# Both score products of an odd step ahead of the second mixing, query transposes in even steps, and half of the block relayouts issued by SyncE

## The chip, the cores and the metric

The kernel runs on one core of a Trainium2 chip. TensorE (PE; PEld is its weight load) multiplies into PSUM, which is eight banks of 128 partitions by 512 float32. VectorE (DVE) and ScalarE (ACT) read PSUM and write the on-chip memory SBUF; GpSimd (POOL) works in SBUF alone. SyncE (SP), ACT and POOL issue the transfers (DMA) between SBUF and the device's main memory or inside SBUF. Each engine works through its own list of instructions in order and waits on semaphores for the others. The metric is the time of one execution in microseconds (us).

## The reference

Attention with mixing of heads before and after the softmax ("talking heads") for 4 batches, 12 heads, 448 positions and head size 64, then a feed-forward layer:

```python
scores = scale * np.matmul(q, k.transpose(0, 1, 3, 2))
scores = np.einsum('bhij,hg->bgij', scores, w_pre)
scores = scores - np.max(scores, axis=-1, keepdims=True)
attn = np.exp(scores)
attn = attn / (np.sum(attn, axis=-1, keepdims=True) + 1e-09)
attn = np.einsum('bhij,hg->bgij', attn, w_post)
attn_out = np.matmul(attn, v)
x = np.ascontiguousarray(attn_out.transpose(0, 2, 1, 3)).reshape(B * S, H * D)
h = x @ w_in
g = s * np.maximum(h, 0.0) ** 2 + b
return g @ w_out
```

`w_in` is 768 by 2048, `w_out` 2048 by 768, x has 1792 rows; all is float32.

## The kernel before, in words

The kernel has an attention stage (steps 0 to 89 of one loop, and a tail) and a feed-forward stage that keeps PE full; the change touches the attention alone.

**Chunks, pairs, blocks.** Each batch's 448 query rows are cut into chunks of 120, 120, 120 and 88 rows: 16 chunks, `ci`. For a chunk and a pair of heads `p` (six pairs), `qk` (line 506) multiplies transposed queries `Tq` by transposed keys `Tk` into two PSUM banks `sc`, and `s_copy` (line 519) has ACT copy them, scaled, into the chunk's score tile `S` in SBUF. A *block* is ten query rows with their twelve heads. `relayout(t)` (line 593) is a DMA that carries block t from `S` (rows on partitions) into a tile `blk`, in which the 120 pairs of row and head lie on partitions. There are eight `blk` tiles, and two blocks (an even t and the odd one after it) make a *step* s.

**A step on PE.** `premix` (line 601) multiplies the step's two blocks by `wpre` into two banks `pm`: the first mixing of heads. DVE takes row maxima (`st`, line 617), ACT the exponentials `e` with their sums (line 623), POOL and DVE make from the sums the weights `W` (lines 629, 634, 636). `postmix` (line 638) of step s-2 multiplies `e` by `W` into two banks `po`, the second mixing, and `evacuate` (line 656) has DVE copy both banks into `A`. In even steps `av` and `av_last` (lines 529, 541) multiply `A` by `v` for two head pairs into `xp`; ACT and DVE copy that out, POOL adds, and SP stores the result `xd` (line 588).

**The odd and the even step.** PE's order in a step is the order of the loop's code: `premix`; `av` (even steps), transposes `tr`, `av_last`; one `qk` of the kind "more" (odd steps); `postmix`; one `qk` of the kind "qk" (odd steps, a few even ones). There are 8 banks in four slots of two: `pm` alternates between slots A and B, `xp` and the "more" scores use the one of A and B that the step before has left, `po` has slot C, and the second `qk` and the transposes share slot D. So `postmix` of a step can begin only when DVE has copied the `po` of the step before, and in an even step `xp` can begin only when ACT has read the odd step's `pm`.

**What sets the order around it.** A table `plan` (lines 667 to 748) gives the step of every `qk`, transpose, `av` and load. Query transposes of a chunk (`tr_q`, line 481) stand in the last odd step that is at least one step ahead of the chunk's first `qk`; key transposes (`tr_keys`) in even steps. The copies of the second `qk` are put off to the head of the next step (list `scopies`). At a step's end the relayouts for step s+4 are issued (LDS is 4), then the loads of the plan, then the stores `xd`. In the stretch before the loop, even blocks go to SP and odd ones to POOL; in the loop all go to POOL's queue. SP issues every other load of the attention stage. Each DMA of SP also waits for the one eight DMAs back on its queue.

Of the kernel before, what the change touches and what calls it, by code (L numbers as in the profile page):

```python
# [22 lines left out]
def talking_heads_attention__then__act_relu2_kernel(  # L23
# [13 lines left out]
    nc = tc.nc  # L37
    B, H, S, D = q.shape
# [4 lines left out]
    NP = H // 2  # L43
# [21 lines left out]
    NCH = len(chunks)  # L65
# [15 lines left out]
    LDS, NBLK, LAG = 4, 8, 2  # L81
# [187 lines left out]
    def one(tag, name):  # L269
        return ps.tile([P, 512], F32, tag=tag, name=name, bufs=1)  # L270

    def slot(tag, name):
        return [one(f"{tag}{i}", f"{name}_{i}") for i in range(2)]

    def next_slot(name):
        tag = slots[turn["slot"] % len(slots)]
        turn["slot"] += 1
        return slot(tag, name)
# [227 lines left out]
    def qk(ci, p, sc):  # L506

        b, n0, n = chunks[ci]
        if p == 0:
            s_t[ci] = sp.tile([CH, H, S], F32, tag=f"S{ci % 3}", name=f"S_{ci}")  # L510
        qt, kt = q_t[ci % 2], k_t[b, p]
        for c0, c1 in ((0, 64), (64, CH)):
            for e in range(2):
                nc.tensor.matmul(  # L514
                    sc[e][c0:c1, :S], qt[64 * e:64 * e + 64, p, c0:c1], kt[64 * e:64 * e + 64, :],
                    start=True, stop=True,
                )

    def s_copy(ci, p, sc, apart=False):
        n = chunks[ci][2]  # L520
        s = s_t[ci]
        if apart:
            nc.scalar.activation(s[:n, 2 * p, :], sc[0][:n, :S], AF.Copy, scale=SCALE)
            nc.vector.tensor_scalar_mul(s[:n, 2 * p + 1, :], sc[1][:n, :S], SCALE)
        else:
            for e in range(2):
                nc.scalar.activation(s[:n, 2 * p + e, :], sc[e][:n, :S], AF.Copy, scale=SCALE)  # L527
# [65 lines left out]
    def relayout(t):  # L593
        ci, r, ni = blocks[t]
        nb = first[ci + 1] - first[ci]
        queue = nc.gpsimd if t >= 2 * LDS or t % 2 else nc.sync
        queue.dma_start(  # L597
            blk_t[t % NBLK][R0:R0 + ni * H, :], s_t[ci][r:r + nb * (ni - 1) + 1:nb, :, :]
        )

    def premix(s):
        pm = pm_t[s] = slot("AB"[s % 2], f"pm_{s}")
        for c in range(2):
            blk = blk_t[(2 * s + c) % NBLK]
            for b in range(2):
                k = slice(0, 64) if b == 0 else slice(64, 64 + U)
                nc.tensor.matmul(  # L607
                    pm[b][64 * c:64 * c + 64, :S], wpre[k, :], blk[k, :], start=True, stop=True
                )
# [17 lines left out]
    def totals(s):  # L627
        e, st = e_t[s]
        nc.gpsimd.tensor_scalar(st[:, 4:6], st[:, 2:4], 1e-9, None, op0=ALU.add)
# [39 lines left out]
    plan = {}  # L669

    def at(step, kind, *what):
        plan.setdefault((step, kind), []).append(what)

    LAST_QK = first[NCH - 1] // 2 - LDS - 1
    where = {}
# [4 lines left out]
    for s in range(1, LAST_QK + 1):  # L680
        for kind in ("more", "qk") if s % 2 else ("qk",):
            if n < len(pairs) and (s % 2 or n < len(pairs) * s / LAST_QK):
                ci, p = where["qk", n] = pairs[n]
# [6 lines left out]
    def place(jobs, room):  # L690
        left = 0
        for s in range(NS + LAG + NP + 1):
            left = room(s, left)
            for job in sorted((j for j in jobs if j[0] <= s), key=lambda j: j[1]):
                lo, hi, cost, key, kind, what = job
                if left > 0 or hi <= s:
                    jobs.remove(job)
                    assert s <= hi, job
                    left -= cost
                    where[key] = s  # L700
                    at(s, kind, *what)
        assert not jobs

    jobs = []
    for ci in range(2, NCH):
        s = where[ci, 0]
        where["tr", ci] = max(s - 2 + (s + 1) % 2, 0)
        at(where["tr", ci], "tr", tr_q, ci, 0, NP)
        b = chunks[ci][0]
        if chunks[ci - 1][0] != b:  # L710
            for p in range(0, NP, 2):
                hi = where[ci, p] - 1
                jobs.append((max(where[ci - 1, p + 1] + 1, hi - 3), hi, 1, ("tr", b, p), "tr", (tr_keys, b, p)))
    place(jobs, lambda s, left: s % 2 == 0)

    jobs = []
    for ci in range(NCH):
# [71 lines left out]
    for p in range(NP):  # L789
        sc = next_slot(f"sc_0_{p}")  # L790
# [10 lines left out]
    for p in range(NP - 2):  # L801
        sc = next_slot(f"sc_1_{p}")
        qk(1, p, sc)
        s_copy(1, p, sc, True)

    scopies = []
    NDONE = NS + LAG
    for s in range(NDONE + NP + 1):
        def todo(kind):
            return plan.pop((s, kind), [])  # L810

        while scopies:
            s_copy(*scopies.pop(0))
        if s == LAST_QK + 1:
            early.close()
            rp = ctx.enter_context(tc.tile_pool(name="rp", bufs=1, side="right", reuse_waits="tile"))
            rp.tile([P, S], F32, tag="xraw", name="place_xraw", bufs=NKC)
            rp.tile([P, X_GAP // 4], F32, tag="gap", name="gap_x", bufs=1)
            rp.tile([P, 2, S], F32R, tag="x", name="place_x", bufs=NKC)
            rp.tile([P, END_GAP // 4], F32, tag="end", name="gap_end", bufs=1)  # L820
        other = "AB"[(s + 1) % 2]
        if s < NS:
            premix(s)
        for _ in range({LAST_QK + 5: 4, LAST_QK + 7: 4, LAST_QK + 9: 4, NS + 1: 3, NS + 2: 3}.get(s, 0)):
            head_piece()
        users = {}

        def take(tag, name):
            for _, f in users.pop(tag, []):
                f()  # L830
            users[tag] = []
            return slot(tag, name)

        outputs = todo("av")
        if outputs:
            assert len(outputs) <= 2
            tag = other if s < NS else "B" if s < NS + LAG else "CB"[s % 2]
            outputs = [(*o, xp) for o, xp in zip(outputs, take(tag, f"xp_{s}"))]
            for output in outputs:
                av(*output)  # L840
        for f, *args in todo("tr"):
            for o, x in f(*args, take("D", f"tr_{s}")):
                turn["copy"] += 1
                i = turn["copy"] % 2
                users["D"].append((1 + i, partial((on_act, on_dve)[i], o, x)))
        if outputs:
            av_last(outputs)
            users[tag] += x_copies(outputs)
        for ci, p in todo("more"):
            tag = "D" if outputs else other  # L850
            sc = take(tag, f"sc_{ci}_{p}")
            qk(ci, p, sc)
            users[tag].append((3, partial(s_copy, ci, p, sc)))
        copies_due = sorted(sum(users.values(), []), key=lambda x: x[0])
        if s < NS:
            open_softmax(s)
            maximum(s, 0)
            if s % 2 == 0:
                exponential(s, 0)
        if 0 <= s - 1 < NS:  # L860
            weights(s - 1)
        if s < NS:
            maximum(s, 1)
        for n, f in copies_due:
            if n < 4:
                f()
        if s < NS:
            if s % 2:
                exponential(s, 0)
            exponential(s, 1)  # L870
        due = 7 * NU_EARLY * (s - CONV0) / (LAST_QK - 2 - CONV0)
        while s % 2 == 0 and turn["ops"] < min(due, 7 * NU_EARLY):
            turn["ops"] += 1
            convert_step(NU_EARLY)
        if LAG <= s < NS + LAG:
            postmix(s - LAG)
            for t in (2 * (s - LAG), 2 * (s - LAG) + 1):
                evacuate(t)
        for ci, p in todo("qk"):
            sc = slot("D", f"sc_{ci}_{p}")  # L880
            qk(ci, p, sc)
            scopies.append((ci, p, sc))
        for n, f in copies_due:
            if n == 4:
                f()
        if s < NS:
            totals(s)
        if s + LDS < NS:
            for t in (2 * (s + LDS), 2 * (s + LDS) + 1):
                relayout(t)  # L890
        for f, *args in todo("load"):
            f(*args)
        store_x(0)
        i = s - LAST_QK - 1
        if 0 <= i < NKC:
            load_x(0, 0, i)
        if 2 <= i < NKC + 2:
            split_x(0, 0, i - 2)
            low_parts()
        for kc in (2 * (i - NKC), 2 * (i - NKC) + 1):  # L900
            if 0 <= kc < NKC:
                load_x(0, 1, kc)
            if 4 <= kc < NKC + 4:
                split_x(0, 1, kc - 4)
                low_parts()
        for _ in range(4 if s >= NS else 0):
            convert_step(NU_EARLY + 3)
# [18 lines left out]
    for r in range(NR):  # L926
# [5 lines left out]
        last = {b: i for i, (b, f) in enumerate(order)}  # L932
# [87 lines left out]
```

## Time and profile before

| | |
|---|---|
| median of 3 runs | 836.83 us (831.28 to 839.35) |
| the profiled execution | 836.27 us, its span 834.6 us |
| PE busy | 814.5 us (98%) |
| DVE, ACT, POOL busy | 533.9, 432.6, 327.6 us |
| chain that ended last | PE 91%, DVE 3%, DMA 2%, "issue" 2%, ACT 1%, POOL under 0.5% |
| attention loop | step 0 at 20.6 us, step 89 at 359.5 us |

Matmuls overlap in the array and their ends are modelled, so PE reads as busy where it only waits inside a run of matmuls; what a stretch costs is read from the starts of its runs. "Issue" is time in which an engine waited for nothing that the profile shows.

### The profile page before, as it was taken

The numbers are of one execution on the slowest core, as the hardware profiler recorded it, in microseconds if no ns is written. First come the engines' busy times: TensorE is split into PE (matmuls) and PEld (weight loads), VectorE is DVE, ScalarE is ACT, GpSimd is POOL, SyncE is SP. The second block draws the span as 40 slices with busy tenths as digits, with TensorE's granted clock in tenths as the row PEclk, the third lists the DMA queues.
The fourth block names the chain that finished last, engine by engine and source line by source line (L and its number), as shares of the span: only waits on it lengthen the run. The fifth ranks groups of instructions, "written<-read, shape, count | busy, mean of one in ns | idle before, by whom it ended". The sixth has DMA issues, their size and how long they took to land.

```text
span 834.6 us, 27353 instructions
## 1 busy us (share of the span) xinstructions
PE 814.5 (98%) x11288; PEld 680.6 (82%) x11288; DVE 533.9 (64%) x1182; ACT 432.6 (52%) x1015; POOL 327.6 (39%) x631
## 2 busy tenths in 40 slices
PE   8988998999999999999999999999999999999998
PEld 4556666666666766689999999999999999999998
DVE  6556677687777787889713999390079329947111
ACT  4755676677667676538687731211186877200000
POOL 4556677587756777725332410000033324100000
PEclk9999999999999999999999999999999999999999
DMA  6998379756994477623422335353114302445331
GB/s 147 218 212 211 125 194 216 180 185 173 225 206 156 148 207 196 212 85 94 158 66 67 83 89 161 118 163 134 42 37 144 104 1 77 149 146 185 97 95 48
DMA packets 116483, 115.88 MB, mean 139 GB/s; under 512 B 67892, under 2 KB 105256, under 8 KB 116360
## 3 DMA queue, kind: packets, MB, share of 16 engines
q1 hardware_dynamic: 92976, 64.79, 29.7%
q0 software_dynamic: 14240, 37.75, 15.6%
q10 hardware_dynamic: 9144, 11.60, 3.9%
q8 instruction: 89, 1.46, 0.7%
q14 instruction: 34, 0.28, 0.1%
HBM read 58.99 MB, written 16.52 MB: 90 GB/s over the span
## 4 chain that ended last, share of the span: by engine, by line
PE 91%; DVE 3%; DMA 2%; issue 2%; ACT 1%; POOL 0%; SPq 0%; DVEq 0%; POOLq 0%
PE po L337 28%; PE ph L289 26%; PE po L650 8%; PE sc L514 7%; PE pm L607 7%; PE xp L536 7%; PE xp L551 2%; PE ph_head L289 1%; DMA blk<-S 1%; DVE A L661 1%; PE tr L457 1%; DMA nk<-in_k_dram 1%; PE tr L488 1%; DVE st L617 1%; PE busy L760 0%
## 5 line engine op out<-in xcount | busy, mean ns | idle before, releaser
L623 ACT ACTIVATE e<-pm,st 128x448 f32<-128x448 f32 x180 | 113.2, 635 | 31.4 <-DVE st L634 27.6
L617 DVE TENSOR_REDUCE st<-pm 128x1 f32<-128x448 f32 x180 | 108.9, 610 | 31.5 <-PE pm L607 14.5
L597 POOL DMA_DIRECT2D blk<-S x176 | 108.0, 614 | 32.1 <-issue 10.2
L650 PEld LDWEIGHTS po<-W,e 60*64 60x64 f32 x5040 | 93.6, 136 | 28.3 <-issue 15.9
L661 DVE COPY A<-po 128x420 f32<-128x420 f32 x180 | 98.4, 588 | 28.5 <-PE po L650 27.6
L527 ACT ACTIVATE S<-sc 120x448 f32<-120x448 f32 (+1 forms) x172 | 84.5, 548 | 44.5 <-PE sc L514 44.2
L650 PE MATMUL po<-W,e 60*64 60x60 f32 x5040 | 99.1, 220 | 7.2 <-issue 6.6
L514 PE MATMUL sc<-Tk,Tq 64*56 64x448 f32 (+1 forms) x768 | 98.8, 549 | 4.0 <-issue 2.5
L607 PE MATMUL pm<-blk,wpre 64*64 64x448 f32 (+1 forms) x720 | 94.3, 546 | 2.4 <-issue 0.9
L337 PE MATMUL po<-w,g 128*128 128x384 f32 x504 | 94.2, 336 | 0.0
L305 POOL TENSOR_TENSOR big<-h,big 128x448 fp32r<-128x448 f32 x24 | 30.8, 1283 | 154.7 <-ACT big L304 154.7
L636 POOL TENSOR_SCALAR W<-kron,st 128x60 f32<-128x60 f32 x180 | 82.1, 469 | 20.2 <-DVE st L634 13.4
L305 POOL TENSOR_TENSOR g<-h,g 128x448 fp32r<-128x448 f32 x40 | 49.1, 1228 | 103.3 <-ACT g L304 92.0
L289 PE MATMUL ph<-x,w 128*128 128x448 f32 x432 | 88.1, 362 | 0.0
L337 PEld LDWEIGHTS po<-w,g 128*128 128x128 f32 x504 | 88.0, 188 | 0.0
L289 PEld LDWEIGHTS ph<-x,w 128*128 128x128 f32 x432 | 81.0, 187 | 5.5
L536 PEld LDWEIGHTS xp<-A,v 128*64 128x64 f32 x1152 | 55.7, 136 | 31.9 <-ACT e L623 19.0
L289 PE MATMUL ph<-x,big 128*128 128x448 f32 x378 | 77.6, 362 | 0.0
L289 PEld LDWEIGHTS ph<-x,big 128*128 128x128 f32 x378 | 70.9, 188 | 4.8
L536 PE MATMUL xp<-A,v 128*64 128x120 f32 (+1 forms) x1152 | 66.0, 263 | 0.6 <-DVE A L661 0.5
L337 PE MATMUL po<-big,g 128*128 128x384 f32 x336 | 65.1, 336 | 0.0
L344 ACT ACTIVATE ob<-po 128x384 f32<-128x384 f32 x28 | 13.8, 493 | 97.8 <-PE po L337 86.1
(89 smaller groups left out, 1252.7 us busy)
## 6 DMA issues: line engine op xcount, KB each, us to landing
blk<-S POOLq DMA_DIRECT2D x168, 210.0 KB, 4.2
raw<-in_moe_w_in_dram SPq DMA_DIRECT2D x32, 384.0 KB
raw<-in_moe_w_out_dram SPq DMA_DIRECT2D x32, 384.0 KB
xraw<-xd SPq DMA_DIRECT2D x48, 224.0 KB
part<-ob ACTq DMA_DIRECT2D x28, 192.0 KB
acc<-part SPq DMA_DIRECT2D x28, 192.0 KB
out_dram<-acc ACTq DMA_DIRECT2D x28, 192.0 KB
xd<-xs SPq DMA_DIRECT2D x72, 60.0 KB
```

Of the source, the lines that this page charges most:

```text
L289: nc.tensor.matmul(ph[:, :S], w[:, i, c0:c0 + P], x[:, y, :], start=(kc == 0 and m == 0), stop=(kc == NKC - 1 and m == 2),)
L337: nc.tensor.matmul(po[:, :NO], g[:, x, c0:c0 + P], w[:, y, :], start=(f == 0 and m == 0), stop=(f == NF - 1 and m == 2),)
L514: nc.tensor.matmul(sc[e][c0:c1, :S], qt[64 * e:64 * e + 64, p, c0:c1], kt[64 * e:64 * e + 64, :], start=True, stop=True,)
L527: nc.scalar.activation(s[:n, 2 * p + e, :], sc[e][:n, :S], AF.Copy, scale=SCALE)
L536: nc.tensor.matmul(xp[64 * e:64 * e + 64, :2 * m].rearrange("q (b n) -> q b n", b=2), vt[:, e, c, :], a[:, c:c + NC:NC - 1, 2 * p + e, :m] ...
L597: queue.dma_start(blk_t[t % NBLK][R0:R0 + ni * H, :], s_t[ci][r:r + nb * (ni - 1) + 1:nb, :, :])
L607: nc.tensor.matmul(pm[b][64 * c:64 * c + 64, :S], wpre[k, :], blk[k, :], start=True, stop=True)
L617: nc.vector.tensor_reduce(out=e_t[s][1][:, b:b + 1], in_=pm_t[s][b][:, :S], axis=AX.X, op=ALU.max, negate=True)
L623: nc.scalar.activation(e[:, b, :], pm_t[s][b][:, :S], AF.Exp, bias=st[:, b:b + 1], accum_out=st[:, 2 + b:3 + b])
L636: nc.gpsimd.tensor_scalar(w[:, b, :], kron2, st[:, 6 + b:7 + b], None, op0=ALU.mult)
L650: nc.tensor.matmul(po[r][64 * c:64 * c + 64, m * U:m * U + U], e[64 * r:64 * r + U, b, j0:j0 + 64], w[64 * r:64 * r + U, b, :], start=True ...
L661: nc.vector.tensor_copy(a_t[ci].rearrange("q m h j -> q (m h) j")[:, :, UI * r:UI * r + UI], po_t[t // 2][t % 2][:, :n].rearrange("q (m i) ...
```

## The change

Three edits. The first: `second(s)`, a function that holds what stood behind `postmix`, is called in odd steps without `av` ahead of the copies and so ahead of `postmix`; in even steps it stays where it was. The second: query transposes go to the last free even step ahead of the chunk's first `qk` (free: no key transposes there, and behind the last use of the buffer). The third: in the whole loop even blocks are issued by SP and odd ones by POOL.

```diff
     def relayout(t):
         ci, r, ni = blocks[t]
         nb = first[ci + 1] - first[ci]
-        queue = nc.gpsimd if t >= 2 * LDS or t % 2 else nc.sync
+        queue = nc.gpsimd if t % 2 else nc.sync
...
         s = where[ci, 0]
-        where["tr", ci] = max(s - 2 + (s + 1) % 2, 0)
-        at(where["tr", ci], "tr", tr_q, ci, 0, NP)
...
+    for ci in range(2, NCH):
+        last = where[ci - 2, NP - 1] if ci > 3 else -1
+        where["tr", ci] = max(
+            s for s in range(last + 1, where[ci, 0]) if s % 2 == 0 and (s, "tr") not in plan
+        )
+        at(where["tr", ci], "tr", tr_q, ci, 0, NP)
...
+    def second(s):
+
+        for ci, p in plan.pop((s, "qk"), []):
+            sc = slot("D", f"sc_{ci}_{p}")
+            qk(ci, p, sc)
+            scopies.append((ci, p, sc))
...
             qk(ci, p, sc)
             users[tag].append((3, partial(s_copy, ci, p, sc)))
+        if s % 2 and not outputs:
+            second(s)
         copies_due = sorted(sum(users.values(), []), key=lambda x: x[0])
...
             postmix(s - LAG)
             for t in (2 * (s - LAG), 2 * (s - LAG) + 1):
                 evacuate(t)
-        for ci, p in todo("qk"):
-            sc = slot("D", f"sc_{ci}_{p}")
-            qk(ci, p, sc)
-            scopies.append((ci, p, sc))
+        if s % 2 == 0 or outputs:
+            second(s)
```

**PE in step 41**, an odd step, from its last `premix` matmul on (`pm_41` is the first mixing, `sc_9_0` and `sc_9_1` two score products of chunk 9, `po_39` the second mixing, 28 matmuls). Before:

```order
L607 MATMUL pm_41_1_3770<-blk3_139,wpre_101 64x448
L514 MATMUL sc_9_0_0_3775<-Tk_2_0_3003,Tq1_135 64x448
L514 MATMUL sc_9_0_1_3776<-Tk_2_0_3003,Tq1_135 64x448
...
L650 MATMUL po_39_0_3794<-W_39_3711,e_39_3619 64x60
L650 MATMUL po_39_1_3795<-W_39_3711,e_39_3619 64x60
...
L514 MATMUL sc_9_1_0_3826<-Tk_2_1_3004,Tq1_135 64x448
L514 MATMUL sc_9_1_1_3827<-Tk_2_1_3004,Tq1_135 64x448
```

and now:

```order
L607 MATMUL pm_41_1_3763<-blk3_139,wpre_101 64x448
L514 MATMUL sc_9_0_0_3768<-Tk_2_0_3013,Tq1_135 64x448
L514 MATMUL sc_9_0_1_3769<-Tk_2_0_3013,Tq1_135 64x448
...
L514 MATMUL sc_9_1_0_3775<-Tk_2_1_3014,Tq1_135 64x448
L514 MATMUL sc_9_1_1_3776<-Tk_2_1_3014,Tq1_135 64x448
...
L650 MATMUL po_39_0_3793<-W_39_3709,e_39_3617 64x60
L650 MATMUL po_39_1_3794<-W_39_3709,e_39_3617 64x60
...
L607 MATMUL pm_42_0_3837<-blk4_140,wpre_101 64x448
```

The second product has moved ahead of the second mixing, whose next neighbour is now the first mixing of step 42.

**SP's queue at the head of the loop** (`blk` rows are relayouts, `nq`, `nk` and `v` loads of queries, keys and values). Before, from the last relayout ahead of the loop on:

```order
L597 DMA blk6_142<-S_0_273 120x1x448
L443 DMA nq_3_535<-in_q_dram 80x4x64
...
L443 DMA nq_3_535<-in_q_dram 8x4x64
L427 DMA nk_1_0_602<-in_k_dram 64x8x64
...
L427 DMA nk_1_1_605<-in_k_dram 64x6x64
L402 DMA v_0_685<-in_v_dram 64x2x256
```

and now:

```order
L597 DMA blk6_142<-S_0_273 120x1x448
L597 DMA blk0_136<-S_0_273 120x1x448
L597 DMA blk2_138<-S_0_273 120x1x448
L443 DMA nq_3_535<-in_q_dram 80x4x64
...
L597 DMA blk4_140<-S_1_429 120x1x448
L443 DMA nq_4_602<-in_q_dram 112x4x64
...
L597 DMA blk6_142<-S_1_429 120x1x448
L427 DMA nk_1_0_676<-in_k_dram 64x8x64
```

Every step has one relayout on SP now, and the loads stand between them; in all, 86 relayouts leave POOL's list and enter SP's. On DVE, ACT and PE no instruction is added or taken away: apart from the second products, only the transposes of 13 chunks and their copies have moved, each from an odd step to an even one.

## Rows read from the trace of the kernel before

**Rows 1.** The page: queue (packets, MB, busy share), chain, POOL issues (us, ns), us to landing.

```profile
q0 software_dynamic: 14240, 37.75, 15.6%
...
PE 91%; DVE 3%; DMA 2%; issue 2%; ACT 1%; POOL 0%; SPq 0%; DVEq 0%; POOLq 0%
...
L597 POOL DMA_DIRECT2D blk<-S x176 | 108.0, 614 | 32.1 <-issue 10.2
...
blk<-S POOLq DMA_DIRECT2D x168, 210.0 KB, 4.2
```

**Rows 2.** Windows: stretch, length, busy time of each engine, granted clock, DMA share, GB/s.

```profile
20.00:58.00 38.00, 34.80 (x706) 20.36 (x700) 23.03 (x52) 25.97 (x69) 21.39 (x48) 1.00 1.03 215
...
80.00:100.00 20.00, 17.53 (x438) 11.83 (x440) 11.43 (x29) 11.05 (x32) 11.52 (x27) 0.91 0.46 137
```

**Rows 3.** Timeline of PE: start, us, line, tile, count; the step starts 86.56 and 328.25.

```profile
86.56 1.10 PE L607 MATMUL pm<-blk,wpre 64*64 64x448 f32 x8
...
328.25 0.94 PE L607 MATMUL pm<-blk,wpre 64*64 64x448 f32 x8
```

**Rows 4.** Timeline of PE, steps 65 and 66, and the start of 67.

```profile
273.88 0.98 PE L607 MATMUL pm<-blk,wpre 64*64 64x448 f32 x8
274.69 0.93 PE L514 MATMUL sc<-Tk,Tq 64*64 64x448 f32 x8
275.44 0.99 PE L650 MATMUL po<-W,e 60*64 60x60 f32 x56
...
277.01 0.93 PE L607 MATMUL pm<-blk,wpre 64*64 64x448 f32 x8
277.87 1.45 PE L536 MATMUL xp<-A,v 128*64 128x120 f32 x24
...
279.53 1.00 PE L650 MATMUL po<-W,e 60*64 60x60 f32 x56
280.37 0.96 PE L607 MATMUL pm<-blk,wpre 64*64 64x448 f32 x5
```

**Rows 5.** The chain that ended last, 86.5 to 328.3 us: its shares by line.

```profile
by line: PE sc L514 20.3%; PE po L650 19.5%; PE pm L607 18.6%; PE xp L536 18.3%; PE xp L551 5.8%; DVE A L661 3.3%; PE tr L457 2.7%; issue 2.4%; PE tr L488 2.1%; DVE st L617 1.3%; DVE Tk L502 0.9%; DVE raw L192 0.8%; DVE xr L502 0.7%; DVE xs
```

**Rows 6.** Timeline of PE and DVE, step 41 and the start of 42.

```profile
180.50 0.98 PE L607 MATMUL pm<-blk,wpre 64*64 64x448 f32 x8
...
182.06 1.31 PE L650 MATMUL po<-W,e 60*64 60x60 f32 x53
...
184.86 1.45 PE L536 MATMUL xp<-A,v 128*64 128x120 f32 x24
...
181.24 1.09 DVE L661 COPY A<-po 128x420 f32<-128x420 f32 x2
```

**Rows 7.** Timeline of ACT, step 65.

```profile
275.67 0.98 ACT L527 ACTIVATE S<-sc 120x448 f32<-120x448 f32 x2 [1.34 <-PE sc L514]
...
277.66 0.22 ACT L623 ACTIVATION_READ_ACCUMULATOR e<-pm,st 128x1 f32 x1
277.75 0.99 ACT L527 ACTIVATE S<-sc 120x448 f32<-120x448 f32 x2
```

**Rows 8.** Timeline of SP's queue: relayouts, and the first and last of its next 16 rows.

```profile
17.07 5.86 SPq L597 DMA_DIRECT2D blk<-S  x4
23.03 4.30 SPq L443 DMA_DIRECT2D nq<-in_q_dram  x6
...
55.76 0.72 SPq L414 DMA_DIRECT2D v<-in_v_dram  x1
```

**Rows 9.** Timeline of SP's queue, the first and last of 20 rows, 132 to 162 us.

```profile
132.88 0.39 SPq L137 DMA_DIRECT2D raw<-in_moe_w_in_dram  x1
...
158.87 3.38 SPq L443 DMA_DIRECT2D nq<-in_q_dram  x6
```

**Rows 10.** The chain that ended last, 20 to 86.6 us: start, us, what.

```profile
36.77 6.95 DMA blk<-S
...
80.68 2.31 issue
```

## What the change does to the time: the prediction

> **What bounds the kernel now.** I began with the chain that ended last on the page: PE holds 91% of it and POOL under 0.5% [rows 1]. A faster POOL is thus worth nothing by itself, and the 108.0 us in which it issues relayouts lie beside PE's work. The feed-forward stage is PE's alone, and the change does not touch it; a gain or a loss in the attention goes through to the end unaltered.
>
> Then the attention, 86.56 to 328.25 us, steps 16 to 79 in the profile [rows 3]. The chain over these 241.7 us holds, beside PE's own lines, 3.3% of DVE's copies `A` (8.0 us), 2.4% of "issue" (5.8 us) and some 4% of other DVE work [rows 5]. So PE is the bound, and DVE's copy of `po` is the largest wait. What that looks like is seen in two pairs of an odd and an even step. In steps 65 and 66 nothing is late: first mixing to next first mixing is 3.13 us in the odd step (273.88 to 277.01) and 3.36 us in the even one, 6.49 us for the pair [rows 4]. In step 41 the second mixing starts at 182.06, while DVE copies the step before's `po` from 181.24 to 182.33; its 53 matmuls spread over 1.31 us, against 0.99 us for all 56 in step 65 [rows 4, 6]. From the first mixing to `xp` of the even step it takes 4.36 us there (180.50 to 184.86) [rows 6] and 3.99 us in step 65 (273.88 to 277.87) [rows 4].
>
> ACT stands close behind. `xp` of the even step takes the slot of the odd step's `pm`, so it waits for the odd step's last exponential: its accumulator is read out by 277.88, and `xp` starts at 277.87 [rows 4, 7]. ACT comes there from the copy of the "more" scores, which starts 1.79 us after the first mixing [rows 7]. This chain is 4.0 us long, whatever PE does between.
>
> **The change part by part.**
>
> *Second product ahead of the second mixing.* No instruction is added. The odd step's second mixing starts 0.75 us later: first mixing 0.81, two products at 0.75 each, so 2.3 us into the step in place of 1.56 (step lengths from the starts in [rows 4]). In step 41 the copy `A` ends 1.83 us into the step (182.33 less 180.50) [rows 6], so it would no longer be waited for. PE's new odd step is 0.81 + 0.75 + 0.75 + 0.83 = 3.14 us, with 0.83 for second mixing to first mixing (279.53 to 280.37 [rows 4]): no shorter than the tight step before. The edit thus pays only where `A` is late, and only down to ACT's 4.0 us: 0.36 us in step 41. Of the 32 odd steps of the stretch, 13 show this picture, with 4.27 to 4.92 us from first mixing to `xp`, transposes aside; those behind a key transpose are the latest, and ACT holds them to about 4.27. Together I read 5 us from them. Bounds: 8 late copies of 1.0 us stand on the chain (8.0 us); if all of it came back, 8.0, and if each gave only step 41's 0.36, 2.9. I take 5, which the steps themselves give.
>
> What is late next: `A` of the odd step is now copied beside the first mixing of the even step, so the even step's first row maximum, behind it on DVE, starts about 0.2 us later. The exponential that waits for this maximum stands on ACT behind the copy of the second scores, which begins only when the odd step's exponentials are done (277.75) and takes 0.99 us [rows 7]; that covers it. Without this cover it would cost 0.2 us in 40 steps, 8 us. The order of these copies on ACT does not change, and slot D, which the second product needs 0.8 us earlier, was emptied at the head of the step before.
>
> *Query transposes in even steps.* The same matmuls and copies, 13 times, at another place: the odd step loses them, the even step gets them. In an even step they delay ACT's and DVE's later work, as key transposes do now, and the following odd step gets 0.2 us longer by ACT's chain. In the odd step before they cost as much. Net 0, between -1 and +2 (0.15 us for each of 13).
>
> *Relayouts on SP.* POOL loses 86 issues of 614 ns [rows 1], 53 us off the chain: 0. A relayout has to land four steps later, some 13 us of which the landing takes 4.2 [rows 1]; in steady steps that covers SP's queue. The place to look at is 23 to 57 us. There SP's 16 rows of loads sum to 32.0 us of the 33.4 between first and last [rows 8], the DMA share is 1.03 [rows 2], and the chain waits on a relayout that takes 6.95 us [rows 10]. Four relayouts took SP 5.86 us, 1.47 each [rows 8]. Nine more are 13.2 us; SP falls 12 us behind by the end, against a cover of four steps of 4.0 us less 6.95 for the landing and 0.9 for the first mixing, 8.2 us. So up to 3.8 us late there. But part of SP's 32 us is itself waiting for full DMA engines, and loads that no longer run ahead leave room for relayouts; the other bound is a gain of 1 us. I take +2.
>
> *Behind the relayout on SP* stand the loads and the stores `xd`. Loads of keys and queries are planned two or three steps ahead of their transposes, 7 to 10 us; a lag of 3 or 4 us in steady steps stays below that. In 132 to 162 us SP's 20 rows sum to 26.0 us of 29.4 [rows 9]; eight relayouts add 11.8 and leave a lag of 8.4 us, below the 11 us of four steps of 4.1 less issue and a landing of 4.2.
>
> Sum: 836.27 (the profiled execution; its span is 834.6) - 5 + 0 + 2 = 833.3. That execution lies 0.6 us below the median of the runs; I say **833**.
>
> **Rivals.**
>
> *Nothing comes back (837 us).* ACT's chain is 4.0 us where PE's new path is 3.14 + 0.86 = 4.0 us: they are equal. If DVE's 0.2 us reaches ACT after all, or the startup's 3.8 us is paid in full, the 5 us are gone: 833.3 + 3.8 = 837. For it: the equality in step 65. Against: 13 late steps have slack to give.
>
> [...]
>
> *The pauses go too (826 us).* PE also pauses where the profile names no wait: 5.8 us in the stretch [rows 5], and 2.31 us at 80.68 [rows 10], after which the granted clock is 0.91 in 80 to 100 us, the lower of its two levels (1.2 GHz) for some 3.6 us (1.8 us lost) [rows 2, 10]. They come while transfers are dense. Smaller packets and another order of loads may thin them out; if two thirds of these 9.9 us went, 833 - 7 = 826. They may as well grow.
>
> *SP becomes the bound (850 us).* If a relayout holds SP for about 1.9 us or more, as the slower of the four may have, SP's queue in 132 to 162 us outgrows its cover: (29.4 - 26.0 + 11) / 8 = 1.8 us is the point from which it decides. At 2.3 us, first mixings wait in the startup (32.0 + 9 x 2.3 - 33.4 - 8.2 = 11 us) and in three stretches like that of [rows 9] (26.0 + 8 x 2.3 - 29.4 - 11 = 4 us, of which half is made up between them): 833 - 2 + 11 + 6, about 850, counting 2 us for a lower clock behind long waits. For it: 1.47 us is a mean with a full queue. Against: SP's queue idles most of the time elsewhere.
>
> **How the numbers follow.** Forecast (830 to 836) 0.48; nothing or ten engines (837) 0.24, of which ten engines 0.10; pauses go (826) 0.16; SP bound (850) 0.12. About 1% (8.4 us) is what a measurement of this kernel tells from no change: the three runs before span 8.1 us. Faster than 828.5 is most of the pauses' case and a little of the forecast: 0.17. Slower than 845.2 is the SP case: 0.12. Between: 0.71. The range leaves out the SP case and the far end of the pauses' case, and takes in the bounds of the gain (8.0) and the startup (+3.8) with pauses 4 us either way: 825 to 842.
>
> **What would show it.** Right: 53 matmuls of the second mixing in odd steps back at 0.99 us or less, `A` under 1% of the chain from step 16 to 79, the first mixing to `xp` near 4.0 us in the 13 steps, step 79 reached 4 to 6 us sooner after step 16. Third edit: SP's relayouts near 1.2 us each, no first mixing waiting for `blk` after 60 us. Wrong: `xp` waiting for ACT by 0.2 us or more in most odd steps, or first mixings that wait for `blk`; step 16 starting over 4 us later than 86.56 means the startup was mis-sized.

## The result: 0.7% slower, and the profile after

The changed kernel takes 840.50 us (median of 20 runs, 832.61 to 844.54), the kernel before 834.29 us in as many runs beside it (830.04 to 839.35): 1.0073 times as long, with a 95% interval of 1.005 to 1.0095. The forecast was 833 us, a gain. The profiled execution has 841.25 us, its span 839.5 us, 4.9 us more than that of before.

The page of the kernel after, with the rows that answer to [rows 1]; for a DMA queue: packets, MB, busy share of 16 engines:

```profile
q0 software_dynamic: 7360, 19.31, 7.5%
...
PE 90%; DMA 5%; DVE 1%; issue 1%; SPq 1%; ACT 1%; POOL 0%; ACTq 0%; DVEq 0%; POOLq 0%
...
L597 POOL DMA_DIRECT2D blk<-S x90 | 58.2, 648 | 34.6 <-issue 16.8
...
blk<-S POOLq DMA_DIRECT2D x86, 210.0 KB, 4.1
```

DVE (3% before) and "issue" (2%) are down to 1% each of the chain that ended last, and transfers have come in: 5% against 2%. The same is read from the chain by line, 86.5 to 330 us of the kernel after, which answers to [rows 5]:

```profile
by line: PE pm L607 20.3%; PE po L650 20.2%; PE sc L514 19.2%; PE xp L536 18.0%; PE xp L551 5.5%; DMA blk<-S 4.4%; PE tr L488 3.3%; PE tr L457 3.1%; DMA nk<-in_k_dram 1.8%; issue 0.9%; DVE A L661 0.5%; DVE xs L502 0.4%; SPq L597 0.4%; POOL
```

The copy `A` fell from 3.3% to 0.5%, so the first edit did what it was to do. What is new are blocks (`blk`) and keys (`nk`). Here are the late transfers in the chain from 60 to 365 us of the kernel after (start, us, what), with SP's own time ahead of the keys; ahead of 60 us, in the stretch of [rows 10], the chain has transfers in both kernels:

```profile
65.23 1.37 SPq L427
...
67.44 5.05 DMA nk<-in_k_dram
...
160.12 0.85 SPq L597
161.69 4.49 DMA nk<-in_k_dram
...
244.15 5.80 DMA blk<-S
...
325.69 4.92 DMA blk<-S
```

Before, no transfer stood in the chain between 43.8 and 360 us. The two transfers of keys follow pieces of SP's own time: they left late. How late the second keys of the batch come is seen in SP's queue. First the loads of keys of step 36 in the kernel before (start, us, engine, line, tile, count):

```profile
151.15 1.56 SPq L427 DMA_DIRECT2D nk<-in_k_dram  x2
...
153.95 2.02 SPq L427 DMA_DIRECT2D nk<-in_k_dram  x2
```

and the same loads after, with what stands around them:

```profile
155.60 0.82 SPq L597 DMA_DIRECT2D blk<-S  x1
156.53 1.30 SPq L427 DMA_DIRECT2D nk<-in_k_dram  x2
157.92 2.11 SPq L588 DMA_DIRECT2D xd<-xs  x2
160.12 0.85 SPq L597 DMA_DIRECT2D blk<-S  x1
161.02 1.85 SPq L427 DMA_DIRECT2D nk<-in_k_dram  x2
```

The second pair of loads leaves 7.1 us later (161.02 against 153.95), about what eight relayouts at 0.85 us take. From 134 us on SP has no gap of over 0.4 us there. PE reaches step 36 2.8 us earlier than before, and in its timeline after stands for 4.68 us in the middle of the key transposes:

```profile
161.12 0.52 PE L457 MATMUL tr<-ident,nk 128*128 128x128 f32 x3 [0.22 <-DMA nk<-in_k_dram]
166.32 1.28 PE L457 MATMUL tr<-ident,nk 128*128 128x128 f32 x5 [4.68 <-DMA nk<-in_k_dram]
```

Behind this stand the granted clock falls. The window of 140 to 180 us (length, busy time of PE, PEld, DVE, ACT, POOL, granted clock, DMA share, GB/s), before and then after:

```profile
140.00:180.00 40.00, 37.48 (x916) 25.42 (x912) 28.56 (x70) 26.22 (x73) 25.88 (x58) 1.00 0.74 193
```

```profile
140.00:180.00 40.00, 35.10 (x853) 24.27 (x845) 26.98 (x67) 24.55 (x71) 18.88 (x45) 0.96 0.65 183
```

The granted clock is 0.96 of full in it: the trace has 3.4 us at the lower level (0.50 of full in a window of 166.3 to 169.6 us) from 166.2 us on, as the wait ends; the same comes at the waits for the keys of step 12 (6.8 us, from 70.7 us on) and for the block of step 58 (3.4 us, from 251.6 us on). That is 13.6 us at half speed in the attention, at most 6.8 us lost (in 2.0 us of them PE stood waiting in any case), against at most 1.7 us before. The trace gives the level as a share, not in GHz; an estimate of the rate comes from the feed-forward stage of the kernel before, where at full clock 672 matmuls of 384 columns take 116.48 us and 576 of 448 columns 115.60: 64 columns more take 27.4 ns, 2.34 columns a ns, and half of that is 1.17.

Step by step, from the first weight load of one first mixing to that of the next, the 4.9 us come about so (us after less us before):

```
start of step 0 to step 16     +0.6   step 12 +5.2 and 13 +1.1 (keys, half clock), step 15 -4.7 (a pause of before is gone)
step 16 to step 79             +0.8   step 36 +6.0 (keys), 57 and 58 +4.6 (block of step 58, half clock);
                                      31, 53 and 76 together -4.2 (pauses gone); the 57 others -5.6
step 79 to step 89             +3.5   step 79 +1.5 (block of step 80), step 82 +2.0 (a pause)
```

So the gain was there, 5.6 us in the steps outside these places, and so were new waits for transfers, which with their half clock cost more than the order and the vanished pauses gave.

### The profile page after: what moved, and what is told of

Read it like the earlier page. It is cut to its first block, busy times and chain, and to the rows that moved or that the text cites. A ratio compares the mean times of both kernels' runs of the same rounds, so it can differ in the third digit from the quotient of the medians.

```text
span 839.5 us, 27309 instructions
## 1 busy us (share of the span) xinstructions
PE 808.8 (96%) x11288; PEld 684.0 (81%) x11288; DVE 530.2 (63%) x1182; ACT 430.3 (51%) x1015; POOL 276.3 (33%) x545
## 4 chain that ended last, share of the span: by engine, by line
PE 90%; DMA 5%; DVE 1%; issue 1%; SPq 1%; ACT 1%; POOL 0%; ACTq 0%; DVEq 0%; POOLq 0%
PE po L337 28%; PE ph L289 26%; PE pm L607 8%; PE po L650 8%; PE sc L514 7%; PE xp L536 7%; DMA blk<-S 3%; DMA nk<-in_k_dram 2%; PE xp L551 2%; PE ph_head L289 1%; PE tr L457 1%; PE tr L488 1%; DMA v<-in_v_dram 1%; SPq L427 1%; PE busy L764 0%
## 5 line engine op out<-in xcount | busy, mean ns | idle before, releaser
L650 PE MATMUL po<-W,e 60*64 60x60 f32 x5040 | 96.3, 221 | 2.7 <-issue 2.7
L607 PE MATMUL pm<-blk,wpre 64*64 64x448 f32 (+1 forms) x720 | 92.6, 552 | 5.7 <-DMA blk<-S 4.7
L636 POOL TENSOR_SCALAR W<-kron,st 128x60 f32<-128x60 f32 x180 | 77.0, 436 | 42.4 <-DVE st L634 36.4
L514 PE MATMUL sc<-Tk,Tq 64*64 64x448 f32 (+1 forms) x768 | 88.1, 541 | 1.3 <-DVE Tq L502 1.3
L597 POOL DMA_DIRECT2D blk<-S x90 | 58.2, 648 | 34.6 <-issue 16.8
L514 PEld LDWEIGHTS sc<-Tk,Tq 64*64 64x64 f32 (+1 forms) x768 | 36.2, 130 | 35.0 <-issue 23.9
```

The source lines that it names most:

```text
L514: nc.tensor.matmul(sc[e][c0:c1, :S], qt[64 * e:64 * e + 64, p, c0:c1], kt[64 * e:64 * e + 64, :], start=True, stop=True,)
L607: nc.tensor.matmul(pm[b][64 * c:64 * c + 64, :S], wpre[k, :], blk[k, :], start=True, stop=True)
L636: nc.gpsimd.tensor_scalar(w[:, b, :], kron2, st[:, 6 + b:7 + b], None, op0=ALU.mult)
L650: nc.tensor.matmul(po[r][64 * c:64 * c + 64, m * U:m * U + U], e[64 * r:64 * r + U, b, j0:j0 + 64], w[64 * r:64 * r + U, b, :], start=True ...
```

## The experiments

**Taking the change apart.** The first kernel has the order and the even transposes without the relayouts on SP (back from the changed kernel):

```diff
-        queue = nc.gpsimd if t % 2 else nc.sync
+        queue = nc.gpsimd if t >= 2 * LDS or t % 2 else nc.sync
```

> The new order and the even-step transposes, with the relayouts back on POOL's queue. Queue theory (SP's queue is full in stretches, so keys and blocks come late; the order itself is a gain): the waits for nk in steps 12 and 36 and for blk in steps 57 and 79 are gone, the copies A stay near 0.5% of the chain from step 16 to 79, time 826 to 831 us, ratio to the kernel before 0.990 to 0.996. Order theory (the order itself costs, by transposes in even steps or a later A): 838 to 842, ratio above 1.003, with waits of xp or pm for ACT or DVE.

Measured: 832.04 us against 833.23, ratio 1.000 (0.9977 to 1.0024). No key is late and blocks are waited for by 0.2 us, and `A` is at 0.2% of its chain; but the time is the old one. The order theory is wrong, and the queue theory's gain is missing. More on that below.

The second has the relayouts on SP and nothing else (the line above, turned round, in the kernel before).

> The kernel before with the 86 relayouts moved to SP and nothing else. Queue theory: the same waits as in the changed kernel (keys 4 to 5 us at the first and second change of batch, blocks 3 us), each followed by a stretch at half clock, without the order's gain: 843 to 849 us, ratio 1.010 to 1.017. Order theory: 833 to 836, no such waits, ratio within 0.002 of 1.

Measured: 839.21 us, ratio 1.0068 (1.0036 to 1.0101). In its profile, the longest of the twelve runs (846.53 us), PE waits 5.6 us for `nk` and 3.0 us for `v`, and only 0.2 us for `blk`. The direction and the waits for keys are as the queue theory has them; its wait for blocks is missing, and the size is 4 us short. By the ratios the relayouts alone cost about all that the whole change costs (1.0068 against 1.0073).

**What stands behind them.** In the third kernel the changed kernel's loads of keys go to POOL's queue:

```diff
-        jobs.append((lo, where["tr", b, p - p % 2] - (3 if p < 4 else 2), 1.0, ("k", b, p), "load", (load_k, b, p)))
+        jobs.append((lo, where["tr", b, p - p % 2] - (3 if p < 4 else 2), 1.0, ("k", b, p), "load", (load_k, b, p, nc.gpsimd)))
```

> The changed kernel with the loads of keys of batches 1 to 3 (44 DMAs) on POOL's queue; the relayouts of even blocks stay on SP. Queue theory (what counts is what stands behind the relayouts on SP): PE's waits for nk fall from 10.6 us to under 3, SP has 44 rows of about 0.7 us less and the waits for blk shrink too: 827 to 833 us. [...]

Measured: 834.25 us, ratio 1.0017 (0.9989 to 1.0045): by the ratios three quarters of the loss are back, and the time is 1.3 us above the range. No transpose `tr` waits for a key, as the queue theory has it; but it has the waits for blocks shrink, and first mixings wait 6.1 us for them, in six places (4.7 us in three places in the changed kernel). The chain of this kernel has two of the blocks:

```profile
235.32 7.91 DMA blk<-S
...
322.04 7.76 DMA blk<-S
```

SP issued the first of them 6 us behind the end of the step that plans it (step 54, which ends at 229.35), after loads of `v` without a gap, and from its issue to its landing it took 7.9 us, against a median of 4.1 us for POOL's on the page above. So lateness has a part in the transfer here too, not only in SP's time.

The next kernel moves the loads of `v` to POOL as well (`load_v, b, p, nc.gpsimd`).

> The changed kernel with the loads of keys and of values of the loop on POOL's queue: SP keeps relayouts of even blocks, queries and stores. Queue theory: first mixings no longer wait for blk (5 us and more with only the keys on POOL, in steps 57 and 79 to 81), little half clock, 829 to 832 us, level with or a little below the kernel with the order alone. Landing theory (SP's relayouts land late by themselves): blk is waited for as before, 834 or more.

Measured: 845.18 us, ratio 1.0147 (1.0118 to 1.0176). Both theories missed it: POOL became what PE waits for. In the waits of PE (what, us in total, times, longest) the second mixing waits for its weights:

```profile
PE po L650 <- POOL W L636: 10.6, 10, 2.1
```

POOL's loads of `v` take 0.6 us each and stand ahead of `W` in its list. Blocks were waited for by 0.2 us only.

Another kernel parts SP's time from the relayout's landing: order alone, relayouts on POOL, and on SP a small copy in each place where the changed kernel has a relayout.

```diff
+    spare = [blkp.tile([P, S // 8], F32, name=f"spare{i}") for i in range(4)]
...
+        if t >= 2 * LDS and t % 2 == 0:
+            nc.sync.dma_start(
+                spare[t // 2 % 4][R0:R0 + ni * H, :], s_t[ci][r:r + nb * (ni - 1) + 1:nb, :, :S // 8]
+            )
```

> The kernel with the order alone and its relayouts on POOL; SP gets, in the places where the changed kernel has its 86 relayouts, copies of an eighth of the same rows into a spare tile that nobody reads. Queue theory, SP's time alone (each about 0.8 us): keys come late in steps 12 and 36 as in the changed kernel, 8 to 12 us of waits for nk and half clock after them, none for blk, 836 to 841 us. Landing theory (the relayouts themselves land late from SP): nothing waits for the spare tile, 831 to 834.

Measured: 843.01 us, ratio 1.010 (1.0067 to 1.0132), 2 us above the range. The copies took SP 826 ns each (median of 86), though they carry an eighth of the bytes; a relayout took 819. PE's waits, first of this kernel, then of the changed one:

```profile
PE tr L457 <- DMA nk<-in_k_dram: 12.4, 5, 5.7
```

```profile
PE tr L457 <- DMA nk<-in_k_dram: 8.9, 4, 4.7
PE pm L607 <- DMA blk<-S: 4.7, 3, 3.4
...
PE xp L536 <- DMA v<-in_v_dram: 2.6, 2, 2.1
```

Nobody reads these copies, and keys are later than in the changed kernel. This is the run that shows the main cause: 86 entries of 120 rows in SP's queue make the keys behind them late, whether each carries 210 KB or an eighth of it. The wait for blocks is not in it (1.0 us against 4.7): there the relayout itself, issued late by the same queue, is what comes late.

**Where the order's gain is.** The next kernel has only the second product moved; transposes stay in odd steps, relayouts on POOL:

```diff
+        where["tr", ci] = max(s - 2 + (s + 1) % 2, 0)
...
-            s for s in range(last + 1, where[ci, 0]) if s % 2 == 0 and (s, "tr") not in plan
```

> Only the second product moved ahead of the second mixing: transposes of queries stay in odd steps, relayouts on POOL. There the transposes and the second product share slot D, so that the product, and the second mixing behind it, wait for the copies of the transposes, about 1 us in 13 steps. If the even-step transposes matter: 4 to 10 us more than the kernel with both edits of the order, with waits of sc for DVE or ACT of some 10 us. If not: the same within 2 us.

Measured: 837.54 us, ratio 1.0071 (1.0042 to 1.0101), 5.5 us above the first experiment. `sc` waits 5.9 us for the copies of the transposes. Without the second edit the first one costs time.

Then the kernel before, with the queues of the third experiment:

> The kernel before with even relayouts on SP and the loads of keys on POOL, so the same queues as the third experiment in the old order. If the order is worth its 5 us: 838 to 840, 4 to 6 us above that experiment. If it is worth as little as with POOL's relayouts: within 2 us of it, 833 to 836.

Measured: 837.66 us, ratio 1.0043 (1.0021 to 1.0065). That is 3.4 us above the new order with the same queues, 2.2 us by the ratios, whose intervals overlap (1.0021 to 1.0065 and 0.9989 to 1.0045): between the two cases, and no verdict.

To see the order without transfers in its way, the next two kernels leave out the relayouts of the loop, one in the old order, one in the new:

```diff
+        if t >= 2 * LDS:
+            return
```

> The kernel before with the relayouts of the loop left out (168 of 176; the first mixings read the old contents of their blocks), so that 16% of the DMA engines' time is gone and PE waits for no block. If PE's pauses without a named wait (steps 15, 31 and 76: 4.1, 2.0 and 1.5 us above the best) come from dense transfers, they shrink to under 1 us together, and the time is 815 to 826 us. If they belong to the instruction list alone, they stay, and the time is 828 to 833.

> The kernel with the order alone, with the same relayouts left out, against the run above it in this list. If the order's gain is real and is eaten by pauses while transfers are dense: 4 to 6.5 us less than that run. If the order gains nothing on the chip and the 5 us of the profiles are chance: within 2 us of it.

Measured: 820.35 us (819.76 to 821.49) and 815.70 us (815.41 to 816.04), a gain of 4.65 us. The runs of one kernel, 8 to 12 us apart with relayouts (12 to 31 runs of either order), now lie within 1.7 and 0.6 us (6 and 5 runs), and from step 16 to 79 no pause shows in the length of a step in either profile. The weight loads of the first mixings of steps 16 and 79, old order, then new (the old order's step 16 is read in two pieces):

```profile
77.81 0.21 PEld L609 LDWEIGHTS pm<-blk,wpre 64*64 64x64 f32 x4 [0.24 <-issue]
...
309.09 0.22 PEld L609 LDWEIGHTS pm<-blk,wpre 64*64 64x64 f32 x8
```

```profile
78.01 0.22 PEld L609 LDWEIGHTS pm<-blk,wpre 64*64 64x64 f32 x8
...
304.88 0.22 PEld L609 LDWEIGHTS pm<-blk,wpre 64*64 64x64 f32 x8
```

231.3 us become 226.9. By pairs of an odd and the next even step:

```
pairs                                                   old order   new order
35, 57 (key transposes beside them)                     16.96       15.53
33, 55 (the same, and they lose query transposes)       18.39       15.55
29, 51 (they get these query transposes)                12.52       13.83
25, 47, 59, 71, 77                                      32.97       31.73
65                                                      6.50        6.50
41                                                      7.20        7.09
the 18 others                                           133.03      132.46
```

Step 16, which gets query transposes now, takes 0.5 us more. The four pairs with key transposes beside them gain 4.3 us, of which pairs 29 and 51 pay 1.3 us back: they have got the query transposes of pairs 33 and 55. That leaves 3.0 us, some 0.7 us for each of the four. Only in pairs 35 and 57 is it the late copy `A`. In step 33 of the old order the second mixing is not late (56 matmuls in 0.99 us); late is the second product, which waits for DVE's copies of the query transposes:

```profile
139.19 0.99 PE L652 MATMUL po<-W,e 60*64 60x60 f32 x56
140.71 0.98 PE L514 MATMUL sc<-Tk,Tq 64*64 64x448 f32 x8 [0.52 <-DVE Tq L502]
```

Step 55 is alike, with a wait of 0.44 us. Both edits have a part in these two pairs, the second by taking the transposes away; how much each gains there was not tried by itself. Five plain pairs gain 0.25 us each, the other 18 some 0.6 us in all, gains and losses mixed, and the tight pair nothing, as its equal paths foretold.

**Why the first experiment shows no gain.** Three more profiles of each order with the relayouts on POOL, without an edit.

> The kernel before once more, for a second profile. In its first one steps 16 to 79 took 238.9 us, of which 232.8 is what each step takes at best in the two profiles with this order, so 6.1 us are pauses without a wait and what follows them. If the order's gain of 5 us is real and hidden by such pauses: again 237 to 241 here. If the first profile was one with more pauses than usual: 233 to 236.

> The kernel with the order alone once more, for a second profile. In its first one steps 16 to 79 took 233.7 us, 226.5 at best by steps. If the order's gain is real and steady: 231 to 236 again. If the first profile had fewer pauses or less half clock than usual, and the new order pauses more (which would explain why its median is only 1 us below that of the kernel before): 236 to 240, with half clock in it.

> A third profile of the kernel before. If the new order pauses more: steps 16 to 79 take 237 to 240 us again (230.2 at best by steps), 7 to 9 us of pauses. If pauses vary alike in both orders: anything from 234 to 247.

> A third profile of the order alone. If the new order pauses more, by the 3 to 4 us that its median lacks: steps 16 to 79 take 235 to 242 us (225.4 at best), 10 to 16 of them pauses and half clock. If the second profile was one odd run: 232 to 235.

> A fourth profile of the kernel before; as for the third: 237 to 240 us if its pauses are steady, 234 to 247 if they vary as in the new order.

> A fourth profile of the order alone; as for the third: 235 to 242 us if the new order pauses more, 232 to 235 if not.

Only one of the three runs that repeat the new order kept the first profile's figure (the first of them, at 242.3 us, lies even above the range for more pauses), and the kernel before was steady. With the first profiles, steps 16 to 79 took, in us:

```
                 first   r1/r2   r3/r4   r5/r6   mean    without relayouts   difference, mean
kernel before    238.9   238.7   240.0   237.7   238.8   231.3                7.5
order alone      233.7   242.3   239.3   234.2   237.4   226.9               10.5
```

Two of the four profiles of the new order are near 234 us, two at 239 and 242. The difference is mostly in pauses of PE without a named wait, and in the half clock behind them. With a spread of 8.6 us among four profiles the 3.0 us by which the new order has more of them in the mean are not clear of chance. The chain of the second profile of the new order (840.60 us) has them:

```profile
80.84 3.35 issue
...
145.05 1.97 issue
...
313.06 4.01 issue
```

The last is step 75, which is 1.9, 6.6, 5.4 and 1.0 us (with step 76) above its best in the four profiles of the new order, step 76 of the old 0.9 to 1.5 us. Half clock follows: 6.8 us long behind the first and third row. Over the timed runs the mean granted clock points the same way: 0.9974 in the new order (12 runs), 0.9986 before (31), 2.2 against 1.2 us lost.

The trace's transfers show what comes just ahead of their ends. The queue that the profile calls "instruction" brings packets of 16 KB, one in 5.0 us on average (50 between 80 and 330 us in the kernel before). Of 22 pauses of over 1 us on the chain between 80 and 330 us in these eight profiles, 21 end 1.25 to 1.74 us after such a packet has landed (the other 0.74), and the packet had begun 4.9 to 9.1 us after the one ahead of it. A stretch of 0.5 us in 5.0 would hold the end of one pause in ten by chance. Still, that is a match in time. What ties it to transfers is that the pauses are gone where relayouts are left out; that the list of instructions is what comes late was not tried by itself.

**A mixed version.** Order alone, even relayouts on SP only in steps in which SP has few loads:

```diff
+        step = t // 2 - LDS
+        calm = step < 0 or step in range(12, 25) or step in range(38, 51) or step in range(60, 73)
+        queue = nc.gpsimd if t % 2 or not calm else nc.sync
```

> The kernel with the order alone; even blocks go to SP only when they are issued in steps 12 to 24, 38 to 50 and 60 to 72, where SP has few loads of keys and values. Queue theory: no added wait for nk or blk; the pause of step 15 gets shorter (it is absent where SP issues relayouts), 828 to 832 us, 0 to 4 below the order alone. If relayouts on SP cost wherever they stand: 834 or more.

Measured: 833.20 us, ratio 0.9979 (0.9946 to 1.0012). Most of the cost of SP's relayouts is gone, so the place matters; a gain can't be told from none. But its profile has what the queue theory ruled out, one added wait for keys, in step 58, and 3.4 us at the lower clock behind it:

```profile
PE tr L457 <- DMA nk<-in_k_dram: 3.1, 1, 3.1
```

SP's last relayout of the calm steps was issued at 216.96 us, and the second keys of step 58 left at 238.69, 5.2 us later than in the first experiment (233.50), with loads between them almost without a gap: the lag was still there 21.7 us after the last relayout. From their issue these keys took up to 6.8 us to land. No version here beats the kernel before clearly.

## Why the prediction was wrong

**The step that failed** is "Behind the relayout on SP". It said that loads are planned 7 to 10 us ahead, and "a lag of 3 or 4 us in steady steps stays below that". Right behind it stands a lag of 8.4 us for 132 to 162 us, which was weighed against the cover of the relayouts alone, 11 us. For the keys in the same queue the cover is 7 to 10 us less a landing of 4 to 5, and that was never subtracted; the sum put this part at nothing. Measured there: a lag of 7.1 us, and 6.0 us lost in step 36; relayouts on SP and nothing else made the kernel 0.68% (5.7 us) slower. The numbers for the right answer stood in the text; the wrong reader of the queue was asked. The relayouts' own cover fell short once as well: in the changed kernel SP issued the block of step 58 at 244.15, 8.8 us behind the end of step 54, it took 5.80 us to land, and the first mixing waited 3.4 us. That "no first mixing" waits for `blk` after 60 us was one of the text's own signs of being right.

**The price of a relayout on SP** was taken as 1.47 us, from four in a full queue. It is 0.82 us. The rival "SP becomes the bound" had its point of decision at 1.8 us and so looked out of reach; by way of the keys the harm came at less than half of that. Its mechanism, SP's queue outgrowing a cover, was the right one; but it named the first mixings (4.7 us of waits) and not the keys (8.9 us), and its 850 us were too high.

**The gain of 5 us** was right in size where nothing is in its way: 4.65 us without relayouts, 5.6 us in the undisturbed steps of the changed kernel's profile. With the relayouts on POOL the timed runs show none of it (ratio 1.000). It lies in part where the text put it, beside key transposes and late copies: 3.0 of 4.4 us in four pairs, 1.2 in five others. In two of the four, what was late was not `A` but the copies of query transposes, which the text did not name. Step 41, the example, was a poor one: from first mixing to `xp` it takes 4.33 us after 4.36, since DVE comes to the row maxima late there. This is the timeline of that step after, PE and then DVE, answering to [rows 6]:

```profile
183.25 1.00 PE L607 MATMUL pm<-blk,wpre 64*64 64x448 f32 x8
184.05 1.83 PE L514 MATMUL sc<-Tk,Tq 64*64 64x448 f32 x16
185.56 1.12 PE L650 MATMUL po<-W,e 60*64 60x60 f32 x53
...
184.55 1.08 DVE L661 COPY A<-po 128x420 f32<-128x420 f32 x2
```

The copies now end at 185.63, as the second mixing starts, but the row maxima of step 41 stand behind them on DVE, and ACT's exponentials wait for these. Step 27 goes from 5.07 to 3.99 us, steps 55 and 33 from 5.6 to 4.2 us (the kernels without relayouts), but all three lose six query transposes too, some 0.8 us of PE's time, which other steps get.

**Query transposes at net 0** held where it can be told, in the runs without relayouts: the two pairs that only lose them gain 1.4 us more than their like (33 and 55 against 35 and 57), and the two that only get them lose 1.3 us. Step 16, which gets them too, takes 0.5 us more. In the eight pairs that move them from the odd to the even step, which gain 1.2 us in all, the two edits can't be told apart.

**The rival "nothing comes back"** (837 us) holds in its outcome for the order with relayouts on POOL (no change that the runs can tell), and by another cause than the one written: without relayouts the gain is there, so ACT's chain did not take it. That pauses did, 3.0 us more of them in the mean, is likely and not shown.

**Ten engines** (837 us, 0.10 of the chances): no run shows how many DMA engines carry a relayout, or which. What the runs show is that the keys come late behind the small copies as well, 12.4 us of waits while all relayouts of the loop run from POOL; and that late blocks from SP took 5.8 us to land in the changed kernel and up to 7.9 us in the third experiment, against a median of 4.1 us from POOL. Why they took longer stays open.

**"The pauses go too"** came half true. With relayouts on SP the pauses of steps 15, 31, 53 and 76 are gone or short, some 9 us in their steps. They were not a net gain, since half clock and waits took their place. Over the timed runs the changed kernel has a mean granted clock of 0.9925, at most 6.3 us lost, against 1.2 us in the kernel before (31 runs beside the first experiment): the half clock at its waits is worth up to 5.1 us of the 6.2 us by which it is slower. The waits themselves come on top, and the order and the missing pauses are set against them.

**The startup at +2** came out at +0.6 us by step 16, by accident: 6.3 us lost to keys in steps 12 and 13, 4.7 won in step 15.

## What to carry to other kernels

When instructions are added to a queue, list everything behind them in it, subtract for each its own cover (planned lead less landing), and let the least cover decide; the entries that are moved need not be the ones that suffer most (PE waited 4.7 us for blocks here, 8.9 us for keys). An entry of 120 rows cost SP's queue 0.82 us here whether it carried 210 KB or an eighth of that, so the bytes did not count, and SP's queue, with 26.0 us of work in 29.4, had no room for eight more: the keys behind them left 7.1 us late. A gain of PE's order is judged on steps without pauses or with the disturbing work left out; one profile of each kernel showed 7.7 us (836.27 against 828.58) where the medians show 1.2.

## What the runs showed that was not expected

- The relayouts bring most of the spread between executions: 0.6 and 1.7 us without those of the loop (5 and 6 runs), 8 to 12 us with them (12 to 31 runs).
- PE's pauses without a named wait end 1.25 to 1.74 us after a 16 KB packet of instructions, in 21 cases of 22. Relayouts issued by SP and not by POOL made four regular ones go; why that is so stays open.
- A relayout from SP is cut into some 119 packets of 1792 bytes, one from POOL into 40 of 5376; by their mean times (89 ns, and 269 to 287 ns) both take about the same engine time, 10.7 and 10.8 to 11.5 us.
- Open as well: why the pauses of step 75 are longer in the new order.
